# Attention and two expert layers on one core: the first batch's gate spread over two more background steps, the first slot's weight load tied to it

## The chip, the cores and the metric

The program runs on one core of a Trainium2 chip. The metric is the device time of one execution in microseconds (us); lower is better. The kernel before was run three times: 547.34, 546.74 and 547.10 us, median 547.1 us.

Engine names: PE is TensorE (PEld its weight loads), DVE is VectorE, ACT is ScalarE, POOL is GpSimd, SP is SyncE, which here issues the DMAs.

## The reference, cut to what matters

For 4 batches (B), 8 heads, 576 positions and head size 64, three layers follow each other:

```
phi(x) = [exp(p), exp(-p)],  p = x @ w_phi - max|x @ w_phi|      # 128 features, 256 with both signs
num = phi(q) @ (phi(k).T @ v);  den = phi(q) . sum_s phi(k);  x1 = num / den

logits = x1 @ w_gate                       # 4 experts, the 2 best of each position are used
x2 = sum over the 2 best e of  w_e * ( causal_softmax(q_e k_e^T / 8) v_e  @ wo_e )

e(s) = argmax of 8 logits, or the expert of the position before where a local gate says so
out = p[e] * relu(x2 @ w1[e]) @ w2[e]
```

The change lies in the first layer's end and in the gate of the second: for each batch the gate finds each position's two best experts of four, counts how often each expert is chosen in the batch, and orders the experts by their counts. The two experts with the highest counts get a full pass over the batch (a "slot").

## The kernel before, in words

**Phase A** computes the first layer. A unit is a batch and a pair of heads: 16 units, unit 4b + p for batch b and pair p. `PhaseA.run` (line 398) has 18 iterations, and iteration i works on three units at once: it projects the keys and queries of unit i (`proj`, line 223, tiles `pjk`, `pjq`, `pje`), makes features, transposes and the key-value product of unit i-1 (`feat_q`, `kv`, `keys`, lines 276 to 307, tiles `tr`, `Y`, `kvt`), and finishes unit i-2 (`num` and `den`, lines 330 and 347, tiles `pn`, `pd`; `den` only in odd iterations). The transposes of `kvtrans` (line 309) of units i-2 and i-1 use the same PSUM bank as `Y`, so that bank must be copied out in turn: line 307 copies Y, line 324 copies its transpose to `kvs`. The order inside an iteration is written out by hand:

```
A_STEPS = ("k0 e0 q0 t x0 f0 t f1 t a kv0 kv1 A t kv2 kv3 t n0 n1 z0 a t t A s0 d0 d1 t")     # line 36
```

Here k, e, q are the projections, x is `kvtrans`, f `feat_q`, kv the key-value product, n `num`, z `feat_k` (the exponentials of the keys on ACT and their sums on POOL), s `keys`, d `den`. Each `t`, and the end of the iteration, is one **tick**. An iteration has nine ticks, so iteration i holds ticks 9i + 1 to 9i + 9.

**Background work.** `Background` (line 69) holds generators in lanes. On each tick, each lane runs one step of its first generator, that is, up to the next `yield`; `yield n` lets the generator sleep until n ticks later, and an entry with `after` waits until the named entry is used up. The lanes of a tick run in the order of their names, "r" before "w". A step that is "held" gets an ordering edge: each of its instructions stands, on its own engine, behind the last anchor of that engine, which for DVE is the last subtraction of `proj` (line 250) and for ACT the last exponential of the features (lines 268, 284).

The code's order is not yet the order on an engine: the build orders the instructions of each engine within the data dependences, the order edges and the waits for buffers. Tiles with one tag share a few buffers in turn; the tag `mm` has two PSUM banks, which `pje`, `pn`, `pd`, the gate's logits (`pg`) and the gate's sum (`pc`) take one after the other.

When unit 4b + 3 is finished, `done(b)` (line 1663) adds to lane "r": `fin{b}` (line 363: store and reload the denominators, a reciprocal on DVE at line 371, reload them spread over the partitions, and eight products on POOL at line 390 that make x1 final) and `gate{b}` (line 1042: store x1 to memory, sleep, `Gates.top2`, store the weights `ws`). For batch 1 it adds to lane "w" the first slot's `early` (line 1174: two indices cast at line 656 and read by SP, two loads `wr` and two loads `wor` at lines 1121 and 1124, then the split of x1[0] into two parts, on ACT at line 1163 and DVE at line 1164) and `cast_w` (line 1126: three pairs of casts, ACT at line 1138 and DVE at line 1139, of the loaded `wr`).

`top2` (line 490) makes the logits in two steps, transposes them in two more, then the maximum, the comparisons (lines 506 to 509), and the choice and its counts `cnt` (lines 512 to 516). After a sleep the matmul at line 519 sums the counts over the partitions into `pc`. The next steps make the total (line 529), the order of the experts (`by_use`, lines 477 to 487, giving `perm`) and the weights in that order (lines 536 and 539, giving `ws`).

The ticks that follow from this:

| Step | Tick before | Iteration, place |
|---|---|---|
| batch 0: logits, first half | 77 | 8, fifth |
| batch 0: counts | 83 | 9, second |
| batch 0: sum `pc` | 85 | 9, fourth |
| batch 0: `perm`, then `ws` | 89, 90 | 9, eighth and ninth |
| slot 0: load, split, casts | 90; 91, 92; 94 to 96 | 9 and 10 |
| `fin1`: first step, reciprocal, products | 93; 97; 102 to 105 | 10 and 11 |
| batch 1: store of x1, logits | 107; 116 | 11; 12, eighth |
| batch 1: counts, sum `pc` | 122; 124 | 13, fifth and seventh |

The first slot's projections with the cast weights begin in iteration 16. **Phases B and C**, the second and third layers, follow phase A and are not touched.

Of the kernel before, what the change touches and what calls it, by code (L numbers as in the profile page):

```python
# [440 lines left out]
class Gates:  # L441
# [5 lines left out]
    def t(self, shape, tag, b, bufs=1, dt=F32):  # L447
        return self.wk.tile([128] + list(shape), dt, tag=tag, name=f"{tag}_{b}", bufs=bufs)
# [41 lines left out]
    def top2(self, xf, wg32, b, out):  # L490
# [10 lines left out]
        w = t([QT, 4], "w4", b)  # L501
# [12 lines left out]
        nc.vector.memset(sel[64:128, 4, :], 0.0)  # L514
        cnt = t([4], "cnt4", b)
        nc.vector.tensor_reduce(cnt, sel.rearrange("p t e -> p e t"), axis=AX.X, op=OP.add)
        yield 2
        pc = ps.tile([128, HALF], F32, tag="mm", name=f"pc_{b}")
        nc.tensor.matmul(pc[:, 0:4], k.ones, cnt, start=True, stop=True)
        nc.vector.tensor_tensor(w, w, sel, op=OP.mult)  # L520
# [490 lines left out]
class PhaseB:  # L1011
# [30 lines left out]
    def gate(self, b):  # L1042
        nc = self.nc
        g = self.g[b] = {}
        nc.sync.dma_start(self.x1d[b], self.x1[b])
        yield 9
        yield from self.gt.top2(self.x1[b], self.wg, b, g)
        nc.sync.dma_start(self.wsd[b], g["ws"])

        t = self.gt.t([2, 4], "ext", b)  # L1050
        nc.vector.tensor_tensor(t, g["hot"][:, 2:4], g["tot"][:, None, :].to_broadcast([128, 2, 4]), op=OP.mult)
        nc.vector.tensor_reduce(self.use[:, b], t, axis=AX.X, op=OP.add)
        nc.vector.tensor_copy(self.ex[:, 1, b], g["perm"][:, 2:4])
        yield
# [573 lines left out]
def kern(tc, kq, v, w_phi, b_gate, wqkv, wo, c_gate, w1, w2, out):  # L1628
    nc = tc.nc
    with ExitStack() as ctx:  # L1630
# [14 lines left out]
        bg = Background(tc)  # L1645
# [10 lines left out]
        with ExitStack() as c2:  # L1656
            ps.pool = c2.enter_context(tc.tile_pool(name="ps_a", bufs=2, space=PSUM, reuse_waits="tile"))
            ps.same = {"tr": ("X", 5), "X": ("X", 5)}
            pa = PhaseA(c2, tc, k, ps, gk, dr, hl, kq, v, w_phi, x1_tile, bg)
            pb.pools(wp, None, ps, None)  # L1660
            slots = pb.slots(order)

            def done(b):
                if b == 1:
                    bg.add("early_" + slots[0].nm, slots[0].early(), lane="w")
                    bg.add("cast_" + slots[0].nm, pb.cast_w(slots[0]), lane="w")
                fin = pa.fin(b)
                bg.add(f"fin{b}", fin, b < B - 1, lane="r", wait=(next(fin) if b == B - 1 else 0))
                bg.add(f"gate{b}", pb.gate(b), lane="r")
                if b == B - 2:  # L1670
                    bg.add("extras", pb.extras(), lane="r")

            pb.fronted = 4
            fronts = iter(range(pb.fronted))

            def after():
                for j in fronts:
                    if j == 0:
                        bg.ensure("cast_" + slots[0].nm)
                    slots[0].front(j)  # L1680
                    break

            def gate_weights():
                for o, w in ((pb, pb.w_gate), (pc, pc.w_gl)):
                    nc.sync.dma_start(o.wg[:, :, 0:w.shape[2]], w)
                    yield

            bg.add("wg", gate_weights())
            pa.run(done, after)
        ps.same = {}  # L1690
        ps.pool = ctx.enter_context(tc.tile_pool(name="ps", bufs=2, space=PSUM, reuse_waits="tile"))
# [66 lines left out]
```

## Time and profile before

| | us |
|---|---|
| median of three runs | 547.1 |
| lowest and highest run | 546.74, 547.34 |
| the profiled execution | 547.5 |
| its span, from first to last instruction | 545.6 |
| PE busy | 524.7 (96% of the span) |
| DVE busy | 362.3 (66%) |
| ACT busy | 263.8 (48%) |
| POOL busy | 157.8 (29%) |

The profile is one execution of the program, recorded by the hardware. Times count from the first instruction. A timeline row gives the start in us, the duration in us, the engine, the line of the kernel, the operation, its output and inputs by name with their shapes, and how many instructions the row merges; a bracket at its end gives the time that the engine sat idle just before, and what released it. Phase A takes about the first 165 us of the span.

### The profile page before, as it was taken

What the parts mean: (1) busy time and instruction counts of PE and PEld (TensorE: products, weight loads), DVE (VectorE), ACT (ScalarE), POOL (GpSimd) and SP (SyncE); (2) the same over time, 40 slices, a digit from 0 to 9 for tenths busy, and PEclk for the clock granted to TensorE, in tenths of its full rate; (3) what the DMA queues carried; (4) which work ended last, traced back from release to release, by engine and by line L of the source; (5) the groups of instructions that cost most, each with busy time, mean ns of one, the idle gap of its engine ahead of it and who ended that gap; (6) DMA issues with size and microseconds to landing.
All of it is one profiled execution on the core that took longest, in us unless ns stands there. A gap on an engine that the chain in (4) does not pass through costs nothing.

```text
span 545.6 us, 11798 instructions
## 1 busy us (share of the span) xinstructions
PE 524.7 (96%) x4456; PEld 439.5 (81%) x4456; DVE 362.3 (66%) x970; ACT 263.8 (48%) x603; POOL 157.8 (29%) x270
## 2 busy tenths in 40 slices
PE   6999999999999999999899999999999999999995
PEld 5776765666667687778667788999999999999995
DVE  7767677977763787968896866852665375617441
ACT  3748466665565466858646553430451135115100
POOL 5574696398468141112445100000000000000000
PEclk9999999999999999999999999999999999999998
DMA  8424364444016023501000601172335133813011
GB/s 245 132 73 127 87 219 135 148 149 157 27 37 217 5 68 115 207 1 55 26 1 2 233 0 31 49 251 107 126 121 193 45 127 122 281 43 126 2 48 46
DMA packets 32709, 57.07 MB, mean 105 GB/s; under 512 B 7012, under 2 KB 17636, under 8 KB 31620
## 3 DMA queue, kind: packets, MB, share of 16 engines
q1 hardware_dynamic: 32644, 56.24, 31.6%
q8 instruction: 37, 0.61, 0.5%
q14 instruction: 28, 0.23, 0.1%
HBM read 41.86 MB, written 14.36 MB: 103 GB/s over the span
## 4 chain that ended last, share of the span: by engine, by line
PE 73%; DVE 10%; ACT 8%; issue 3%; DMA 2%; POOL 2%; SPq 0%; ACTq 0%; DVEq 0%; POOLq 0%
PE po_c L64 6%; PE po_c L65 6%; PE po_c L66 6%; PE pq_s L724 6%; PE ph_c L64 5%; PE ph_c L66 5%; PE ph_c L65 5%; PE Y L295 4%; PE pd L357 3%; PE py_s L870 3%; PE pn L340 3%; PE pt_s L843 2%; PE pjk L242 2%; PE pg L458 2%; ACT a_kp L267 2%
## 5 line engine op out<-in xcount | busy, mean ns | idle before, releaser
L1441 ACT ACTIVATE h_c<-ph_c 128x288 fp32r<-128x288 f32 x64 | 26.0, 409 | 106.3 <-PE ph_c L66 106.0
L64 PE MATMUL ph_c<-xh_c,w1h_c 128*128 128x288 f32 x256 | 76.7, 300 | 0.0
L64 PE MATMUL po_c<-h_c,w2h_c 128*128 128x288 f32 x256 | 76.2, 298 | 0.0
L66 PE MATMUL ph_c<-xh_c,w1l_c 128*128 128x288 f32 x256 | 75.5, 296 | 0.3 <-DVE w1l_c L1394 0.3
L65 PE MATMUL ph_c<-xl_c,w1h_c 128*128 128x288 f32 x256 | 75.7, 296 | 0.0
L65 PE MATMUL po_c<-h_c,w2h_c 128*128 128x288 f32 x256 | 75.5, 295 | 0.0
L66 PE MATMUL po_c<-h_c,w2l_c 128*128 128x288 f32 x256 | 75.4, 294 | 0.0
L272 POOL TENSOR_TENSOR zs<-a_kp 128x256 f32<-128x256 f32 x64 | 47.6, 759 | 56.0 <-ACT x L345 29.0
L1442 DVE SCALAR_TENSOR_TENSOR h_c<-ph_c,h_c 128x288 fp32r<-128x288 f32 x64 | 28.9, 454 | 34.1 <-ACT h_c L1441 33.6
L64 PEld LDWEIGHTS ph_c<-xh_c,w1h_c 128*128 128x128 f32 x256 | 48.1, 188 | 1.6 <-issue 0.9
L64 PEld LDWEIGHTS po_c<-h_c,w2h_c 128*128 128x128 f32 x256 | 48.2, 188 | 0.9 <-issue 0.9
L66 PEld LDWEIGHTS ph_c<-xh_c,w1l_c 128*128 128x128 f32 x256 | 48.0, 188 | 0.9 <-issue 0.5
L65 PEld LDWEIGHTS ph_c<-xl_c,w1h_c 128*128 128x128 f32 x256 | 48.1, 188 | 0.0
L66 PEld LDWEIGHTS po_c<-h_c,w2l_c 128*128 128x128 f32 x256 | 48.1, 188 | 0.0
L65 PEld LDWEIGHTS po_c<-h_c,w2h_c 128*128 128x128 f32 x256 | 48.1, 188 | 0.0
L1464 DVE TENSOR_TENSOR fo_c<-po_c,pb 128x288 f32<-128x288 f32 x32 | 14.5, 455 | 45.3 <-PE po_c L66 45.2
L724 PE MATMUL pq_s<-xh_b,w_s 128*128 128x288 f32 x192 | 43.7, 305 | 0.7 <-DVE q_s L691 0.7
L295 PE MATMUL Y<-a_kp,a_v 128*64 128x256 f32 x320 | 39.3, 385 | 1.0 <-ACT qp L328 0.5
L340 PE MATMUL pn<-qp,kvs 128*64 128x288 f32 x256 | 35.9, 408 | 0.3 <-ACT qp L328 0.3
L267 ACT ACTIVATE a_kp<-uk 128x1024 f32<-128x1024 f32 x30 | 31.5, 1052 | 7.3 <-DVE uk L250 4.1
L724 PEld LDWEIGHTS pq_s<-xh_b,w_s 128*128 128x128 f32 x192 | 32.0, 188 | 3.1 <-issue 1.5
L284 ACT ACTIVATE qp<-tr 128x512 f32<-128x512 f32 x64 | 33.6, 634 | 1.3 <-PE tr L282 1.3
(315 smaller groups left out, 1218.2 us busy)
## 6 DMA issues: line engine op xcount, KB each, us to landing
w1raw_c<-in_w_dram SPq DMA_DIRECT2D x16, 512.0 KB, 4.2
w2raw_c<-in_w_dram SPq DMA_DIRECT2D x16, 512.0 KB, 4.5
raw<-in_kq_dram SPq DMA_DIRECT2D x15, 320.0 KB, 3.1
rb<-d SPq DMA_DIRECT2D x32, 144.0 KB, 3.4
x1d<-x SPq DMA_DIRECT2D x4, 1152.0 KB
x2d<-x SPq DMA_DIRECT2D x4, 1152.0 KB
raw<-in_kq_dram SPq DMA_DIRECT2D x16, 256.0 KB, 3.8
a_v<-in_v_dram SPq DMA_DIRECT2D x16, 256.0 KB, 4.1
```

What stands on the lines that cost most here:

```text
L64: nc.tensor.matmul(out, lh, rh, start=start, stop=False, **kw)
L65: nc.tensor.matmul(out, lh, rl, start=False, stop=False, **kw)
L66: return nc.tensor.matmul(out, ll, rh, start=False, stop=stop, **kw)
L267: nc.scalar.activation(kp[:, 0:4, sg, :], u[:, 0:4, :], AF.Exp, scale=sc)
L272: add(zs[:, j, sg, :], kp[:, j, sg, :], kp[:, 2 + j, sg, :], op=OP.add)
L284: self.bg.anchor(nc.scalar.activation(qp[:, h, sg, 0:512], tp, AF.Exp, scale=sc))
L295: self.kv_last = nc.tensor.matmul(Y[64 * h:64 * h + 64, 0:256], vt[:, t, h, :], kp[:, t, :, h * NF:(h + 1) * NF], start=t == 0, stop=t == 4)
L340: nc.tensor.matmul(pn[64 * h:64 * h + 64, :], kvs[:, sg, 64 * h:64 * h + 64], qp[:, h, sg, c], start=sg == 0, stop=sg == 1)
L357: nc.tensor.matmul(pd[32 * h:32 * h + 32, :], r["kvs"][:, 2, o:o + 32], r["qp"][:, h % 2, sg, c], start=sg == 0, stop=sg == 1)
L724: self.nc.tensor.matmul(out, self.wqkv[t][:, wj, ch, 0:m], x[:, ch, c], start=wj == ch == 0 and x is xh, stop=wj == 1 and ch == 3)
L1441: nc.scalar.activation(hh[:, c], ph, AF.Relu),
L1442: nc.vector.scalar_tensor_tensor(hl[:, c], ph, 0.0, rd(hh[:, c]), op0=OP.max, op1=OP.subtract))
```

## The change

Three lines change. Batch 0's gate sleeps four ticks instead of two between its counts and their sum. The first slot's `early` gets an `after` on gate 0, so it starts in the tick in which that gate is used up, where it had started on its own in tick 90. Batch 1's gate sleeps seven ticks instead of nine after its store of x1.

```
 # Gates.top2
         nc.vector.tensor_reduce(cnt, sel.rearrange("p t e -> p e t"), axis=AX.X, op=OP.add)
-        yield 2
+        yield 2 if b else 4
         pc = ps.tile([128, HALF], F32, tag="mm", name=f"pc_{b}")
         nc.tensor.matmul(pc[:, 0:4], k.ones, cnt, start=True, stop=True)
 # PhaseB.gate
         nc.sync.dma_start(self.x1d[b], self.x1[b])
-        yield 9
+        yield 7 if b == 1 else 9
         yield from self.gt.top2(self.x1[b], self.wg, b, g)
 # kern, done(b)
                 if b == 1:
-                    bg.add("early_" + slots[0].nm, slots[0].early(), lane="w")
+                    bg.add("early_" + slots[0].nm, slots[0].early(), lane="w", after=["gate0"])
                     bg.add("cast_" + slots[0].nm, pb.cast_w(slots[0]), lane="w")
```

The ticks after the change, where they differ:

| Step | Before | After |
|---|---|---|
| batch 0: sum `pc` | 85 | 87 |
| batch 0: total, order of the experts (three steps) | 86, 87 to 89 | 88, 89 to 91 |
| batch 0: `ws`; its store and the last small steps; used up | 90; 91; 92 | 92; 93; 94 |
| slot 0: load | 90 | 94 |
| slot 0: split, two steps | 91, 92 | 95, 96 |
| slot 0: casts, three steps | 94, 95, 96 | 98, 99, 100 |
| `fin1`: first step; reciprocal; products | 93; 97; 102 to 105 | 95; 99; 104 to 107 |
| batch 1: store of x1 | 107 | 109 |
| batch 1: logits and all that follows | 116 | 116 |

## Rows read from the trace of the kernel before

**Rows 1.** The page's first part: engine, busy us, share of the span, instructions

```profile
PE 524.7 (96%) x4456; PEld 439.5 (81%) x4456; DVE 362.3 (66%) x970; ACT 263.8 (48%) x603; POOL 157.8 (29%) x270
```

**Rows 2.** Busy time by stretch: length, then PE, PEld, DVE, ACT, POOL, clock, DMA

```profile
90.00:100.00 10.00, 8.99 (x98) 5.05 (x96) 9.02 (x33) 7.33 (x15) 7.59 (x11) 1.00 0.31 92
...
100.00:110.00 10.00, 9.96 (x109) 7.41 (x105) 9.80 (x22) 7.18 (x15) 1.10 (x2) 1.00 0.65 199
```

**Rows 3.** Waits of PE, 80 to 140 us: total us, times, longest

```profile
PE pc L519 <- DVE cnt L516: 1.0, 1, 1.0
PE pje L242 <- DVE x L343: 0.6, 1, 0.6
```

**Rows 4.** Timeline of PE, 93 to 100 us: start, us, instruction [idle before]

```profile
93.58 0.94 PE L242 MATMUL pjk<-a_w,raw 64*128 64x128 f32 x12
95.49 0.39 PE L519 MATMUL pc<-cnt,ones 128*128 128x4 f32 x2 [0.96 <-DVE cnt L516]
95.80 2.16 PE L340 MATMUL pn<-qp,kvs 128*64 128x288 f32 x16
...
100.06 0.49 PE L242 MATMUL pjk<-a_w,raw 64*128 64x128 f32 x4
```

**Rows 5.** Timeline of PE, batch 1's pc in iteration 13

```profile
140.47 0.39 PE L519 MATMUL pc<-cnt,ones 128*128 128x4 f32 x2
```

**Rows 6.** Timeline of DVE, 97 to 111 us

```profile
97.39 0.61 DVE L485 TENSOR_TENSOR u<-hot,iota 128x16 f32<-128x16 f32 x1
...
98.34 0.19 DVE L656 CAST ri_b<-perm 1x1 int32<-1x1 f32 x2
...
99.14 0.46 DVE L359 TENSOR_SCALAR dn<-pd 128x288 f32<-128x288 f32 x1 [0.24 <-PE pd L357]
100.20 0.46 DVE L359 TENSOR_SCALAR dn<-pd 128x288 f32<-128x288 f32 x1 [0.60 <-PE pd L357]
...
104.97 1.27 DVE L250 TENSOR_TENSOR uq<-pjq,mxq 128x512 f32<-128x512 f32 x2
...
107.05 2.08 DVE L1164 TENSOR_TENSOR xl_b<-x,xh_b 128x576 fp32r<-128x576 f32 x3
109.06 1.28 DVE L1139 TENSOR_TENSOR w_s<-wr_s,w_s 128x512 fp32r<-128x512 f32 x2
110.26 0.45 DVE L343 COPY x<-pn 128x288 f32<-128x288 f32 x1
```

**Rows 7.** Timeline of PE, 110 to 112 us

```profile
110.76 0.37 PE L242 MATMUL pje<-a_w,raw 64*128 64x128 f32 x1 [0.63 <-DVE x L343]
...
111.85 0.44 PE L318 MATMUL kvt<-ident,ue 128*128 128x128 f32 x2
```

**Rows 8.** Timeline of ACT, 102 to 113 us

```profile
102.82 0.49 ACT L324 ACTIVATE kvs<-kvt 128x384 f32<-128x384 f32 x1 [4.80 <-PE kvt L323]
...
104.48 1.29 ACT L1163 ACTIVATE xh_b<-x 128x576 fp32r<-128x576 f32 x2
...
106.58 1.20 ACT L1138 ACTIVATE w_s<-wr_s 128x512 fp32r<-128x512 f32 x2
...
110.41 0.64 ACT L1138 ACTIVATE w_s<-wr_s 128x512 fp32r<-128x512 f32 x1
110.93 0.49 ACT L307 ACTIVATE kvt<-Y 128x384 f32<-128x384 f32 x1
112.65 0.49 ACT L324 ACTIVATE kvs<-kvt 128x384 f32<-128x384 f32 x1 [1.23 <-PE kvt L323]
```

**Rows 9.** Timeline of SP's DMA issues near 100 us

```profile
100.49 0.90 SPq L1121 DMA_DIRECT2D wr_s<-in_wqkv_dram  x2
```

**Rows 10.** The tile wr_s: its eight loads, from issue to landing

```profile
DMA to landing us min/median/max: 3.1/3.3/3.7
```

**Rows 11.** Timeline of POOL (GpSimd), 127 us

```profile
126.97 1.55 POOL L390 TENSOR_TENSOR x<-x,rb 128x288 f32<-128x288 f32 x2
```

**Rows 12.** Timeline of PE, batch 1's logits

```profile
129.08 1.18 PE L458 MATMUL pg<-x,b_wg 128*32 128x288 f32 x16
```

More of the change, by code (lines that the diff above doesn't have):

```diff
@@ L516, in top2 @@
         nc.vector.tensor_reduce(cnt, sel.rearrange("p t e -> p e t"), axis=AX.X, op=OP.add)
-        yield 2
+        yield 2 if b else 4
         pc = ps.tile([128, HALF], F32, tag="mm", name=f"pc_{b}")
@@ L1045, in gate @@
         nc.sync.dma_start(self.x1d[b], self.x1[b])
-        yield 9
+        yield 7 if b == 1 else 9
         yield from self.gt.top2(self.x1[b], self.wg, b, g)
@@ L1664, in done @@
                 if b == 1:
-                    bg.add("early_" + slots[0].nm, slots[0].early(), lane="w")
+                    bg.add("early_" + slots[0].nm, slots[0].early(), lane="w", after=["gate0"])
                     bg.add("cast_" + slots[0].nm, pb.cast_w(slots[0]), lane="w")
```

## The prediction, made before the changed kernel was run

> **What bounds the kernel now.** Read the page's first part first: TensorE (PE) is busy for 524.7 of the 545.6 us span [rows 1], so a change pays only where it removes a wait of PE, and the 20.9 us without PE work are all there is. The profiled execution took 547.5 us: its span and 1.9 us around it, 0.4 us above the median of 547.1. The sum below is made against 547.5 and then carried to the median.
>
> Next, the table by stretches. The change touches batch 0's gate and what follows it, and these lie at 90 to 110 us: PE 8.99 and 9.96 of 10 us, VectorE (DVE) 9.02 and 9.80 [rows 2]. DVE is nearly full too, so what PE waits for there is DVE. The list of waits names PE's only two large ones between 80 and 140 us: 1.0 us for the counts (cnt, line 516) and 0.6 us for a PSUM copy (line 343) [rows 3].
>
> PE's timeline shows the first. Instructions don't stand in the code's order: the build orders each engine's list. Twelve of unit 10's sixteen key matmuls come at 93.58, ahead of unit 7's numerators (pn), since pn takes the `mm` bank after the sum's (pc). PE idles 0.96 us before pc at 95.49; pn follows at 95.80, and the last four key matmuls at 100.06 [rows 4].
>
> **The change, step by step.** Iteration i of phase A holds ticks 9i+1 to 9i+9; batch 0's counts are made in tick 83.
>
> *Step 1: pc from tick 85 (between the products of keys and values) to tick 87 (after pn).* pn now asks for its bank first, and its inputs are there, so its 2.1 us run while DVE finishes cnt. The key matmuls go back behind; nothing is added. Gain 0.96 us; bounds 0 (a new wait for the same cnt) and 0.96. The nearest row for the new place is batch 1's pc, already issued from its iteration's seventh tick: no idle time of PE before it [rows 5]. Can DVE follow? It idles 0.24 and 0.60 us just before unit 10's reductions, and the last of the gate's small steps (perm, ws, the two index casts), 97.39 to 98.53, fill 1.14 us [rows 6]. These go to ticks 91 to 94, where a held step stands behind unit 10's last subtraction, so DVE has 0.84 + 1.14 us to give and PE's 0.96 us stand: that subtraction ends about 105.2 instead of 106.2.
>
> The Trainium skill (Trace Analysis, "Identifying Performance Opportunities") says to look for gains on the engine with the highest occupancy. Over this stretch DVE nearly ties with PE, and by that rule step 1 would be worth DVE's idle time alone, some 0.84 us. The idle rows agree with the size; no run here separates 0.84 from 0.96.
>
> *Step 2: x1's split from ticks 91, 92 to 95, 96; the weight casts from 94 to 96 to 98 to 100.* In the old order unit 8's PSUM copy (line 343, 110.26) stands behind four subtractions of the split and two of the casts: the three at 107.05 and the two at 109.06 alone take 2.08 + 1.28 us [rows 6]. PE idles 0.63 us for it at 110.76 [rows 7]. In the new order only two split subtractions are ahead of it: about 105.2 + 1.1 (moved gate work) + 1.4 + 0.45 = 108.2, before PE asks (110.13 - 0.96 = 109.2). Gain 0.63; bounds 0 and 0.63.
>
> *Step 3: what is late next, ScalarE (ACT).* Unit 9's transposes (line 318) began at 111.85 [rows 7], just behind ACT's copy of Y (line 307), 110.93 to 111.42, which must drain that bank. ACT ran without a hole from unit 8's kvs copy at 102.82 to the end of that copy, 8.6 us, with two split copies (1.29) and three casts (1.20 + 0.64) among it [rows 8]. In the new order all four split copies (2.58) and no cast stand in this run, so it is 0.55 us shorter, and it starts 0.96 earlier: it ends at 111.42 - 0.96 - 0.55 = 109.9 if no hole opens. But the second pair of split copies (tick 96) now stands directly ahead of the copy, behind the key exponentials, where before one cast of 0.64 did, so the end may slip by as much as 1.29 - 0.64 = 0.65, to 110.55. PE would come at 111.85 - 1.59 = 110.26. The bounds of the wait are so 0 and 0.3; I take 0.25, near the upper, since the split copies rank ahead of that copy in the code.
>
> *Step 4: the loads.* Slot 0's load goes from tick 90 to 94. Its index casts ended at 98.53; the two `wr` loads took SP from 100.49 to 101.39, the second begun about 2.4 us after the casts [rows 9], and land 3.1 to 3.7 us after issue [rows 10]. From the end of the subtraction: 105.2 + 1.14 to the casts + 2.4 to the second load + 3.1 to 3.7 = 111.8 to 112.4. On SP, behind the wait for the index, stand slot 0's four loads, batch 1's denominators (tick 95 instead of 93) and unit 13's load, which PE wants in iteration 13; the denominators go into DVE's reciprocal of tick 99 (97 before). I price SP at 0 to PE. The slots' first use of the weights is in iteration 16: 0. Unit 9's kvs copy (ACT, 112.65 with 1.23 us idle ahead of it [rows 8]) is wanted at once by PE. If the casts stay behind it, 0: ACT then has the query copies and casts to do before PE needs unit 9's products copied, and the next iteration is the light kind. If not, rival B.
>
> *Step 5: batch 1.* Its fin moves two ticks, its gate's store of x1 as much (109 for 107), its logits stay in tick 116. The store's bytes are unchanged and the loads behind it in SP are for units 14 and 15: 0, with the margin in rival D.
>
> **Sum:** -0.96 - 0.63 + 0.25 = **-1.3 us**: 546.2 for the profiled execution, **545.8** against the median. After phase A nothing else changes; the later waits are set by the same engines and move along.
>
> **Rivals.**
>
> *A: only one of the two waits goes.* If the build leaves the second pair of split subtractions ahead of line 343's copy as well, PE waits there as before and step 2 is worth 0. Step 3 then takes nothing, since PE comes later: -0.96, **546.1**. For it: DVE and ACT are full here [rows 2, 8], so work that is moved four ticks stands in front of something. Against: the new ticks lie, in the code, behind the copies that PE wants.
>
> *B: the weight casts stop ACT; slower.* Ticks 98 to 100 come ahead of iteration 11's kvs copy in the code. If the build puts the casts there, ACT's list stands until the weights land (111.8 to 112.4), then runs one to three casts of 0.6 us, then kvs. One cast gives kvs at 112.4 to 113.0 against 112.65 now, about no change; two give 113.0 to 113.6 and three 113.6 to 114.2, a loss of 1.0 to 1.6: **548.1 to 548.7**. From the second cast on the kernel is slower than before. (The same casts' subtractions, ahead of unit 11's reductions on DVE, would hold PE's products of unit 9 by as much.) For it: the old order put a cast ahead of the Y copy at 110.41 [rows 8]. Against: the build had the freedom to leave them to the next iteration.
>
> *C: nothing moves.* pc is still early for cnt, or the hole comes back as another wait: **547.1**.
>
> *D: batch 1's logits wait for GpSimd.* The last scaled half of x1 ends at 128.52 [rows 11], PE's logits start at 129.08 [rows 12]. The margin is 0.56; GpSimd's work moves with ACT's products, so mostly 0, but one pair of products (1.55) put later costs 1.55 - 0.56 = 1.0 of what was won: **546.8**.
>
> **How the numbers follow.** About 0.2% (1.1 us) is what a measurement of this kernel can tell from no change: faster means under 546.0, slower over 548.2. Forecast 0.46 (545.8, its own range 545.5 to 546.2; of it 0.41 faster, 0.05 same), A 0.22 (0.03 faster, 0.19 same), B 0.20 (0.15 slower, 0.05 same), C 0.06 and D 0.06 (same). That makes faster 0.44, same 0.41, slower 0.15. The range runs from the whole 1.59 us less half the spread of the three runs (0.3) to B with three casts at the early landing and a little more: 545.2 to 548.2.
>
> **What would show it.** Step 1: pn directly after the products, pc without idle time, unit 10's key matmuls unsplit. Step 2: no wait of PE for line 343. Step 3: PE's wait, if any, is at line 318 for line 307, under 0.4 us. Step 4: the `wr` loads near 108.5, casts behind kvs. It is wrong if ACT shows a wait for wr ahead of kvs (B), if pc still idles (C), or if PE waits for line 390 (D); and if the time goes outside 90 to 135 us, the order of some other stage has changed, which I have not priced.

## The result and the profile after

The changed kernel took 551.1 us (median of five runs, 550.75 to 552.41), beside 547.34 us for the kernel before on the same chip (five runs, 546.74 to 547.88): a ratio of 1.0066, with an interval of 1.0046 to 1.0085. It is **slower by 0.66%, 3.8 us by the medians**. The forecast was 1.3 us faster, and the range ended at 548.2.

The page's first part, the row that answers to [rows 1] (engine, busy us, share of the span, instructions), and the granted clock in 40 slices of the span:

```profile
PE 525.4 (96%) x4456; PEld 439.5 (80%) x4456; DVE 363.9 (66%) x970; ACT 263.6 (48%) x603; POOL 157.3 (29%) x270
...
PEclk9999999979999999999999999999999999999999
```

The span grew from 545.6 to 549.3 us, by 3.7 us. The sums of the engines hardly differ (PE +0.7 us, with the same 4456 instructions), so the reader has to look along the span. One slice stands out, the ninth (109.9 to 123.6 us): its digit of the granted clock is 7, and all others are 9.

**Where the time went** is best read from PE's own marks. Each column below runs from the first row of a group on PE's timeline to the first of the next: the second half of batch 0's logits (pg), the first key matmul (pjk) of units 11, 12 and 13, and the first matmul of the second layer (pq).

| us | pg to unit 11 | unit 11 to 12 | 12 to 13 | 13 to pq | pg to pq | pq to the end |
|---|---|---|---|---|---|---|
| before | 23.53 | 12.09 | 9.79 | 33.87 | 79.28 | 381.54 |
| changed | 22.35 | 17.40 | 9.79 | 33.87 | 83.41 | 381.49 |

So the change won 1.18 us up to unit 11, lost 5.31 in the one iteration behind it, and did nothing to the rest. The sum is +4.13. With -0.38 ahead of the first mark, where the change does nothing, and -0.05 behind the last, that is the span's 3.70 us.

PE's timeline through these stretches (start us, us, instruction, idle time before it and what ended it), the rows that answer to [rows 4, 7]:

```profile
92.74 2.11 PE L340 MATMUL pn<-qp,kvs 128*64 128x288 f32 x16
...
95.32 0.39 PE L519 MATMUL pc<-cnt,ones 128*128 128x4 f32 x2
...
106.75 1.16 PE L242 MATMUL pjk<-a_w,raw 64*128 64x128 f32 x16
...
109.51 0.44 PE L318 MATMUL kvt<-ident,ue 128*128 128x128 f32 x2 [0.48 <-ACT kvt L307]
...
111.81 0.63 PE L282 MATMUL tr<-ident,uq 128*128 128x128 f32 x4 [1.09 <-DVE uk L250]
114.95 4.53 PE L295 MATMUL Y<-a_kp,a_v 128*64 128x256 f32 x20 [2.52 <-ACT qp L328]
119.27 2.65 PE L340 MATMUL pn<-qp,kvs 128*64 128x288 f32 x16
...
124.15 1.16 PE L242 MATMUL pjk<-a_w,raw 64*128 64x128 f32 x16
```

The two waits aimed at are gone: pn stands ahead of pc, pc has no idle time, and line 242 no longer waits for line 343. In their place stand 1.09 us for DVE and 2.52 us for ACT. The twenty matmuls behind them, Y at 114.95, take 4.53 us; the same twenty took 2.38 in the iteration before, at 102.15. ACT's timeline, the rows that answer to [rows 8], shows the 2.52:

```profile
108.96 0.50 ACT L307 ACTIVATE kvt<-Y 128x384 f32<-128x384 f32 x1
112.52 1.67 ACT L1138 ACTIVATE w_s<-wr_s 128x512 fp32r<-128x512 f32 x3 [3.06 <-DMA wr_s<-in_wqkv_dram]
114.10 0.47 ACT L324 ACTIVATE kvs<-kvt 128x384 f32<-128x384 f32 x1
114.47 0.43 ACT L328 ACTIVATE qp<-kvt 128x128 f32<-128x128 f32 x2
```

All three weight casts stand ahead of unit 9's kvs copy, and ACT does nothing for 3.06 us until the weights land. The kvs copy starts at 114.10, where it started at 112.65 before. The load itself, on SP's timeline (it answers to [rows 9]; the last row is the store of batch 1's reciprocals, which stands behind slot 0's four loads):

```profile
107.71 0.90 SPq L1121 DMA_DIRECT2D wr_s<-in_wqkv_dram  x2
...
110.09 0.53 SPq L373 DMA_DIRECT2D d<-cr  x1
```

DVE's timeline, which answers to [rows 6], shows the 1.09:

```profile
103.84 1.27 DVE L250 TENSOR_TENSOR uq<-pjq,mxq 128x512 f32<-128x512 f32 x2
...
105.70 0.20 DVE L656 CAST ri_b<-perm 1x1 int32<-1x1 f32 x2
105.83 1.41 DVE L1164 TENSOR_TENSOR xl_b<-x,xh_b 128x576 fp32r<-128x576 f32 x2
107.16 0.44 DVE L343 COPY x<-pn 128x288 f32<-128x288 f32 x1
...
108.56 2.50 DVE L1164 TENSOR_TENSOR xl_b<-x,xh_b 128x576 fp32r<-128x576 f32 x2
110.98 0.68 DVE L250 TENSOR_TENSOR uk<-pjk,mxk 128x512 f32<-128x512 f32 x1
...
113.18 1.79 DVE L1139 TENSOR_TENSOR w_s<-wr_s,w_s 128x512 fp32r<-128x512 f32 x2 [0.93 <-ACT w_s L1138]
```

The index casts come 7.4 us later than before (98.34 to 105.70), because the step that holds them now lies in iteration 10 and stands behind unit 10's last subtraction (uq, 103.84). The second pair of the split stands ahead of unit 11's uk, and takes 2.50 us where the first pair took 1.41.

Last, the granted clock. The view by stretches (length; busy us of PE, PEld, DVE, ACT and POOL; then clock, DMA share, GB/s):

```profile
110.00:112.00 2.00, 0.91 (x9) 0.70 (x8) 2.00 (x3) 0.00 (x0) 2.00 (x3) 1.00 1.05 342
112.00:114.00 2.00, 0.43 (x4) 0.19 (x2) 1.07 (x2) 1.48 (x3) 1.74 (x3) 0.89 0.85 275
114.00:116.00 2.00, 1.05 (x6) 0.67 (x8) 2.00 (x6) 2.00 (x7) 0.00 (x0) 0.50 0.50 176
116.00:118.00 2.00, 2.00 (x14) 1.05 (x12) 2.00 (x5) 0.84 (x2) 0.87 (x2) 0.50 0.71 226
118.00:120.00 2.00, 2.00 (x12) 1.18 (x10) 1.35 (x3) 1.19 (x2) 0.68 (x1) 0.50 0.24 73
120.00:122.00 2.00, 2.00 (x20) 0.92 (x20) 0.03 (x1) 1.72 (x4) 0.00 (x0) 0.91 0.78 177
```

PE is busy 0.91 and 0.43 of 2 us, and then the clock stands at 0.50, the lower of its two levels (1.2 GHz), until about 120 us. Y and pn are issued in that stretch. From the start of Y to the end of pn, 114.95 to 119.27 + 2.65 = 121.92, they take 6.97 us; before, 113.53 to 117.85, 4.32. That is 2.65 us for the same 36 matmuls. PE's timeline of the kernel before:

```profile
113.53 2.38 PE L295 MATMUL Y<-a_kp,a_v 128*64 128x256 f32 x20
115.74 2.11 PE L340 MATMUL pn<-qp,kvs 128*64 128x288 f32 x16
```

So the +5.31 us of the iteration come apart in three: from unit 11's first matmul to the start of Y 8.20 us instead of 5.22 (+2.98), the clock +2.65, and a smaller gap behind pn (-0.32).

### The profile page after: what moved, and what is told of

Read it like the earlier page. It is cut to its first block, busy times and chain, and to the rows that moved or that the text cites. A ratio compares the mean times of both kernels' runs of the same rounds, so it can differ in the third digit from the quotient of the medians.

```text
span 549.3 us, 11798 instructions
## 1 busy us (share of the span) xinstructions
PE 525.4 (96%) x4456; PEld 439.5 (80%) x4456; DVE 363.9 (66%) x970; ACT 263.6 (48%) x603; POOL 157.3 (29%) x270
## 4 chain that ended last, share of the span: by engine, by line
PE 78%; DVE 7%; ACT 7%; issue 3%; DMA 3%; POOL 2%; SPq 0%; ACTq 0%; POOLq 0%; DVEq 0%
PE po_c L64 6%; PE po_c L65 6%; PE po_c L66 6%; PE pq_s L724 6%; PE Y L295 5%; PE ph_c L64 5%; PE ph_c L66 5%; PE ph_c L65 5%; PE pn L340 3%; PE py_s L870 3%; PE pd L357 3%; PE pjk L242 3%; PE pt_s L843 2%; PE pg L458 2%; ACT a_kp L267 2%
## 5 line engine op out<-in xcount | busy, mean ns | idle before, releaser
L295 PE MATMUL Y<-a_kp,a_v 128*64 128x256 f32 x320 | 41.4, 401 | 3.6 <-ACT qp L328 3.2
L295 PEld LDWEIGHTS Y<-a_kp,a_v 128*64 128x64 f32 x320 | 22.7, 142 | 17.6 <-ACT qp L328 7.0
```

Source lines behind the costliest of these rows:

```text
L295: self.kv_last = nc.tensor.matmul(Y[64 * h:64 * h + 64, 0:256], vt[:, t, h, :], kp[:, t, :, h * NF:(h + 1) * NF], start=t == 0, stop=t == 4)
```

## The experiments

The theory after this reading was: the bound load is late, the casts stand ahead of kvs on ACT, PE's wait is long, and the wait also lowers PE's clock. The rivals were that DVE alone would hold PE, that the clock costs nothing of its own, and that batch 1's gate, begun two steps sooner, is what loses. Each experiment is an edit of the changed kernel unless another base is named. Where marks are given, they are those of the table above. `wait=n` in an edit holds an entry back until n ticks after the one in which it is added, tick 89.

### The casts alone put later

```
-                    bg.add("cast_" + slots[0].nm, pb.cast_w(slots[0]), lane="w")
+                    bg.add("cast_" + slots[0].nm, pb.cast_w(slots[0]), lane="w", wait=14)
```

> The changed kernel, with slot 0's three weight casts asked for nine ticks after the load (tick 103) instead of from tick 98 on; the order of ACT differs only in that. Theory T (the casts stand ahead of unit 9's kvs copy on ACT and hold it until the weights have landed; PE idles, then its clock falls): kvs follows PE's transposes at once, PE's 2.5 us wait and the 2.65 us of half clock go. What stays is the gain at pc and PE's 0.5 and 1.1 us waits at lines 318 and 282: about 547.1, 546.3 to 547.7. Rival U (the loss comes from DVE, where the split's second pair stands ahead of unit 11's subtraction): PE's 1.1 us wait grows and the time stays above 549.

Measured: 548.23 us (ten runs, 546.98 to 550.06) beside 547.62; ratio 1.0009, interval 0.9997 to 1.0022. Against the changed kernel's 1.0066 that undoes most of the loss, though not down to the range expected. PE's timeline of this run:

```profile
111.92 0.63 PE L282 MATMUL tr<-ident,uq 128*128 128x128 f32 x4 [1.07 <-DVE uk L250]
112.48 2.38 PE L295 MATMUL Y<-a_kp,a_v 128*64 128x256 f32 x20
...
129.27 1.43 PE L458 MATMUL pg<-x,b_wg 128*32 128x288 f32 x10 [0.83 <-POOL x L390]
```

Y starts at 112.48, has no wait for ACT and takes 2.38 us; the granted clock is 1.00 in every 2-us stretch from 110 to 122. Unit 11 to 12 takes 12.14 us instead of 17.40. So the casts ahead of kvs are the loss of that iteration. DVE's 1.07 us is still there, and Y nevertheless starts 1.05 us sooner than in the kernel before (113.53).

What is left is new: unit 12 to 13 takes 11.60 us instead of 9.79, because the logits of batch 1 wait for GpSimd: from their first matmul to unit 13 it takes 2.92 us (127.71 to 130.63) where it took 1.11. The chain begins on POOL's timeline. The products with the reloaded reciprocals start only at 117.81, after 3.86 us of waiting for their data:

```profile
117.81 2.09 POOL L390 TENSOR_TENSOR x<-x,rb 128x288 f32<-128x288 f32 x2 [3.86 <-DMA rb<-d]
```

The small store of the reciprocals is issued at 110.23, behind slot 0's four loads, and SP then waits 2.3 us for its landing before it may reload them. In the changed kernel the same products start at 117.13 and cost nothing, since PE itself is some 4 us late there. This is the prediction's rival D: covered in the changed kernel, real as soon as the first loss is gone.

### Casts of data that are ready

Slot 0's casts read the finished x1 of batch 0 in place of the loaded weights, so they don't wait for the load; slot 0's output is then that of other weights.

```
                 src = s.wr[:, :, :, 64 * t:64 * t + 64].rearrange("p j c d -> p c j d")
+                if nm == "s0":
+                    src = self.x1[0][:, :, 0:384].rearrange("p c (j d) -> p c j d", j=2)[:, :, :, 64 * t:64 * t + 64]
```

> The changed kernel in its own order of instructions, but slot 0's casts read x1 of batch 0, which is in place, instead of the loaded weights (slot 0 computes with other numbers, so the output is not the reference's). The loads still run. T: the casts run at about 109.5 to 111.2 and kvs at about 111.2 instead of 114.1, so Y of unit 10 waits for its transposes alone; clock stays at 1.0; 547.0 to 547.8. Rival W (it is the three casts' own 1.7 us on ACT, or their place, not the waiting for the load): kvs late by 1.7 us and more, 549 or above.

Measured: 550.15 us (four runs), ratio 1.0044, interval 1.0028 to 1.0061. **A miss.** kvs starts at about 110.9 as foreseen, and ACT's wait is gone, but PE waits for DVE instead:

```profile
113.96 0.66 PE L282 MATMUL tr<-ident,uq 128*128 128x128 f32 x4 [1.57 <-DVE uk L250]
114.54 3.84 PE L295 MATMUL Y<-a_kp,a_v 128*64 128x256 f32 x17
```

On DVE's timeline two of the casts' subtractions now follow the second pair of the split, all ahead of unit 11's uk:

```profile
108.53 2.49 DVE L1166 TENSOR_TENSOR xl_b<-x,xh_b 128x576 fp32r<-128x576 f32 x2
110.94 2.36 DVE L1141 TENSOR_TENSOR w_s<-x,w_s 128x512 fp32r<-128x512 f32 x2
113.23 0.68 DVE L250 TENSOR_TENSOR uk<-pjk,mxk 128x512 f32<-128x512 f32 x1
```

Y starts at 114.54 instead of 114.95, and the clock falls here as well (0.68, then 0.50 from 116 to 118). So a loss of this kind comes without the wait for the load, from the place of the casts alone: held by the load they stop ACT, and not held they fill DVE at the same place. The prediction had this second path in brackets under rival B.

### PE kept busy in the gap

Unit 10's query transposes are repeated, two and four times in all, so that PE has work while it would wait.

```
-        for t in range(4):
+        for t in list(range(4)) * ((2, 4)[h] if i == 10 else 1):
```

> The changed kernel, with the query transposes of unit 10 done over again (the first four twice, the second four four times, same result), so that PE has some 2 us of work in the hole ahead of unit 10's Y; the wait of ACT for the weights is untouched. T with the clock as a part of the loss: granted clock stays near 1.0 after the hole, Y takes 2.4 us instead of 4.5, and the time falls by 1.5 to 2.7 us to 548.4 to 549.6. If the half clock comes from elsewhere or costs nothing: no change, 550.7 to 551.6.

Measured: 551.06 us (four runs), ratio 1.0063, interval 1.0045 to 1.0081: no gain in the total that the runs can tell. The price of the clock is seen all the same. PE's timeline and the view by stretches:

```profile
115.88 2.38 PE L295 MATMUL Y<-a_kp,a_v 128*64 128x256 f32 x20 [1.35 <-ACT qp L328]
118.09 2.11 PE L340 MATMUL pn<-qp,kvs 128*64 128x288 f32 x16
```

```profile
114.00:116.00 2.00, 0.65 (x7) 0.41 (x7) 1.89 (x3) 2.00 (x7) 0.63 (x1) 1.00 0.51 185
116.00:118.00 2.00, 2.00 (x20) 1.35 (x22) 2.00 (x7) 1.77 (x4) 0.00 (x0) 1.00 0.64 211
```

Y starts later than in the changed kernel (115.88 instead of 114.95), and Y and pn are still done sooner (at 120.20 instead of 121.92): they take 4.32 us at a clock of 1.00, exactly what they took before the change, against 6.97. From pg to pq the stretch takes 81.22 us, 2.19 less than the changed kernel's 83.41. In the profiled run 1.1 us of that are given back behind pq (382.59 instead of 381.49); of it, 0.68 us is a wait at 224 us for a split copy on ACT (line 1163) that the changed kernel's profile does not show. Behind pq, where the code is the same in all, this record's thirteen traces range from 381.49 to 383.09, so 1.1 us there need not come from this edit. So the local cost of the clock is shown, and that its removal lowers the total is not.

### Batch 1's gate put back

```
-        yield 7 if b == 1 else 9
+        yield 9
```

> The changed kernel with the third edit undone: batch 1's gate sleeps nine ticks again, so its logits and what follows come two ticks later than before. T: the loss was made before tick 109, so 550.5 to 551.7. Rival V (the shorter sleep of batch 1's gate costs, through its store or its logits waiting for GpSimd): at least 1 us faster, 550 or below.

Measured: 552.65 us (four runs), ratio 1.0091, interval 1.0074 to 1.0108. That is above the range expected and not below it, so the third edit is not the loss. Without it the stretch from unit 12 to pq takes 44.76 us instead of 43.66, and the logits come later and with a wait:

```profile
136.26 1.18 PE L458 MATMUL pg<-x,b_wg 128*32 128x288 f32 x16 [0.89 <-DVE ue L250]
```

The two steps taken from that sleep keep the gate in its old ticks once `fin1` has moved by two. What they are worth is not shown: unit 11 to 12 is 1.07 us shorter here (16.33 instead of 17.40, with a clock that falls less, to 0.57 and 0.58), so pg to pq takes 83.45 us against 83.41. The totals of this run and of the changed kernel overlap in their intervals.

### The binding alone

The kernel before, with the second edit only.

```
-                    bg.add("early_" + slots[0].nm, slots[0].early(), lane="w")
+                    bg.add("early_" + slots[0].nm, slots[0].early(), lane="w", after=["gate0"])
```

> Edit: the kernel before with only the second edit of the change, slot 0's load bound to the first gate. T (the binding is what moves the casts ahead of kvs): all three casts in a row ahead of unit 10's kvs copy, PE idle there by 2 us or more, the granted clock below 1.00 behind it; 549 to 551 us. Rival U (the binding costs only together with the later counts): casts find their data, kvs late by at most 0.6, 547.0 to 548.0.

Measured: 550.66 us (five runs, 548.86 to 552.98), ratio 1.0053, interval 1.0033 to 1.0074: as expected. The load, the index casts and the casts move by two ticks only, from 90 to 92, but that takes them from iteration 9 into iteration 10. There the index casts stand behind unit 10's last subtraction on DVE (106.24 us instead of 98.34), and the load is issued at 108.53 instead of 100.49. This run's timelines of ACT and then of PE:

```profile
114.34 1.67 ACT L1138 ACTIVATE w_s<-wr_s 128x512 fp32r<-128x512 f32 x3 [3.40 <-DMA wr_s<-in_wqkv_dram]
115.92 0.47 ACT L324 ACTIVATE kvs<-kvt 128x384 f32<-128x384 f32 x1
```

```profile
116.77 3.91 PE L295 MATMUL Y<-a_kp,a_v 128*64 128x256 f32 x20 [3.50 <-ACT qp L328]
```

The clock is 0.50 from 118 to 120 us. From unit 11 to the last twelve key matmuls of unit 12 (four went ahead, at 112.57) it takes 16.77 us against 12.09 before, and from pg to pq 83.86 against 79.28. One `after` of two ticks gives a loss of this size by itself, and with nothing won ahead of it. Note DVE: here it waits 2.84 us itself, and both of unit 11's uk subtractions are done in time. So DVE's 1.09 us of the changed kernel is beside the point, and ACT's stop is enough.

The trace is of an execution of 552.70 us, 2.0 above the median. The five differ in their mean granted clock as they do in time: 548.86 us at 0.999, 550.66 and 550.58 at 0.996 and 0.995, 552.70 and 552.98 at 0.994 and 0.992. The first, whose clock is as high as the kernel before has it, is 1.1 us above the 547.76 us of the kernel before, which is the size that the prediction gave to rival B.

The first edit has no run without the second, since `early` on its own starts in tick 90 and reads the weights `ws`, which the first edit moves from tick 90 to 92.

### The changed kernel again

> The changed kernel, unaltered, on the same chip as the runs of this group, to have its trace a second time. T: three casts ahead of unit 10's kvs, first pjk of unit 12 about 17.4 us behind that of unit 11 (12.1 in the kernel before), granted clock at 0.50 for some us around 116; 550.7 to 551.8 us.

Measured beside the last one: 551.87 us (four runs, 551.7 to 553.62), ratio 1.0084, interval 1.0069 to 1.0099, just above the range, with the same waits (unit 11 to 12 in 17.95 us, Y at 115.64 after 3.04 us for ACT, and a clock of 0.57, 0.50, 0.50 and 0.72 from 114 to 122). The whole change is no faster than its second edit alone, although its first wins 1.2 us ahead of unit 11.

### Load, split and casts all put a unit later, on both kernels

If the preparation of slot 0 only has to be away from units 10 and 11, putting it a unit later should keep steps 1 and 2 and lose nothing. In ticks of the changed kernel, this edit puts the load from 94 to 103, one iteration later at the same place, and the casts from 98 to 113, one iteration and six ticks later; the same waits on the kernel before put them from 90 and 94 to the same ticks. On the changed kernel:

```
-                    bg.add("early_" + slots[0].nm, slots[0].early(), lane="w", after=["gate0"])
-                    bg.add("cast_" + slots[0].nm, pb.cast_w(slots[0]), lane="w")
+                    bg.add("early_" + slots[0].nm, slots[0].early(), lane="w", after=["gate0"], wait=14)
+                    bg.add("cast_" + slots[0].nm, pb.cast_w(slots[0]), lane="w", wait=24)
```

> Edit: the changed kernel with slot 0's load (and with it the split) 14 background steps later and its casts 24 steps later, so that all of it falls one unit later, at the same place within the unit, and the load stands on SyncE behind the reciprocals rb of the second batch instead of ahead of them. Theory T (the changed kernel loses because slot 0's preparation stands in the wrong places: casts ahead of unit 10's kvs copy, the load in flight beside the reciprocals' way): no cast ahead of kvs of unit 10 or 11, GpSimd's first multiply by rb starts at 113 to 115 (117.1 in the changed kernel, 117.8 with the casts alone later), no wait of the second batch's logits for GpSimd, first pjk of unit 12 at 118.5 to 119.3, clock 1.00 throughout; 545.8 to 546.8 us, about 0.25% faster than before. Rival P (GpSimd's own work and not the load sets the second batch's logits): the wait of 0.8 us at the logits stays, 547.4 to 548.2. Rival Q (unit 13's input loads, now behind slot 0's load on SyncE, are late): PE waits for raw at pjk of unit 13, 548 or more.

and the same two waits on the kernel before:

> Edit: the kernel before with slot 0's load and split 14 steps later and its casts 24 steps later; its first batch's counts and the second batch's gate stay where they were. T: the wait of 0.96 us at pc stays, the 0.63 us at pje for the x copy goes, first pjk of unit 12 at 119.7 to 120.2; 546.5 to 547.3 us, so the run above is faster than this one by 0.5 to 1 us. Rival S (the counts' later place is worth nothing, all of the gain is in slot 0's places): equal to the run above within 0.3 us.

Measured: 548.68 us (eleven runs), ratio 1.0019, interval 1.0009 to 1.0029; and 549.05 us (twelve runs), ratio 1.0022, interval 1.0008 to 1.0037. **Both are misses.** They differ by 0.37 us, less than the 0.5 expected, and their intervals overlap, so they do not show what the counts' later place is worth. In the first, unit 11 to 12 takes 10.44 us instead of 12.09, and the next two stretches pay for it, with 12.55 and 35.42 us. PE's waits there:

```profile
119.57 0.37 PE L242 MATMUL pje<-a_w,raw 64*128 64x128 f32 x1 [0.98 <-DVE dn L359]
...
128.44 0.31 PE L304 MATMUL Y<-zs,ones 128*32 128x128 f32 x3 [1.22 <-POOL zs L274]
...
132.60 0.37 PE L242 MATMUL pje<-a_w,raw 64*128 64x128 f32 x1 [1.47 <-DVE lg L459]
```

The waits of 0.98 and 1.47 us are the old line 343's kind: a PSUM bank that DVE has not emptied, with subtractions of the preparation ahead on DVE (those of the split at 117.06 take 2.09 us, a single one of a cast at 125.01 takes 2.78). So the preparation has a price here too.

### The load behind the reciprocals, the casts late

Next, two arrangements that use what was learnt. The first puts the split where the change has it (one tick sooner, since the load no longer takes the tick ahead of it), the load at tick 104 instead of 94, behind the reciprocals' round trip, and the casts at 130 instead of 98:

```
         def early():
+            if b == 0:
+                yield from self.split(lambda ch: self.x1[b][:, ch, :], q, f"b{b}", s.xs)
+                yield 8
             self.load_w(...)
             yield
-            yield from self.split(lambda ch: self.x1[b][:, ch, :], q, f"b{b}", s.xs)
+            if b:
+                yield from self.split(lambda ch: self.x1[b][:, ch, :], q, f"b{b}", s.xs)
...
-                    bg.add("cast_" + slots[0].nm, pb.cast_w(slots[0]), lane="w")
+                    bg.add("cast_" + slots[0].nm, pb.cast_w(slots[0]), lane="w", wait=41)
```

> Edit: the changed kernel, with slot 0's split where the change put it, but its load behind the second batch's reciprocals rb on SyncE and its casts three units later (unit 13 in place of unit 10). Theory T2 (two prices make up the loss: the casts ahead of unit 10's kvs with the slow clock behind it, and the load, in flight while the reciprocals make their round trip, which makes GpSimd's multiplies late): with both removed the 1.2 us won at the counts are kept. Expected: pc and the x copy without a wait, first pjk of unit 11 at 22.3 to 22.4 us behind the first pg (as in the changed kernel), first multiply by rb by 115, no wait at the second batch's logits, first pjk of unit 13 at 43.8 to 44.6 us behind the first pg (45.4 before, 46.1 with the casts alone later, 49.5 in the changed kernel); 546.2 to 547.0 us, 0.1 to 0.3% below before. Rival P2 (GpSimd's own work is the limit, whenever the load comes): the wait at the logits stays at 0.5 us or more, 547.3 to 548.2. Rival C2 (the casts cost as much in unit 13 as elsewhere): a wait of 1 us or more behind them, 547.5 or more.

Measured: 547.11 us (twelve runs), ratio 0.9996, interval 0.9983 to 1.0009. From pg to unit 13 it takes 44.13 us, inside the range expected and 1.28 us less than before (45.41), with no wait at the logits. The wait for the x copy of line 343, expected to stay away, is there (0.75 us at 108.89). The rest gives 0.94 back and puts the total just above its range: unit 13 to pq takes 34.81 us, and PE waits 0.86 us for uk at 154.53, beside the three casts that now follow each other at 147 to 152 us.

### The split two units later, too

The second keeps the load ahead of the split: the load at tick 103, the split at 121, the casts at 130, which are iterations 11, 13 and 14:

```
-            yield
+            yield 18 if b == 0 else 0
...
-                    bg.add("early_" + slots[0].nm, slots[0].early(), lane="w", after=["gate0"])
-                    bg.add("cast_" + slots[0].nm, pb.cast_w(slots[0]), lane="w")
+                    bg.add("early_" + slots[0].nm, slots[0].early(), lane="w", after=["gate0"], wait=14)
+                    bg.add("cast_" + slots[0].nm, pb.cast_w(slots[0]), lane="w", wait=41)
```

> Edit: as the run above, with the split, too, two units later than in the changed kernel, in unit 12, so that units 10 and 11 hold no preparation of slot 0 at all. T2 with GpSimd as the next limit: units 11 and 12 begin about 1.6 us sooner than in the run above, but GpSimd's eight multiplies by rb then stand ahead of unit 12's sums and PE waits for those by 1 to 2.5 us, so that the logits come no sooner than 128.2: first pjk of unit 13 at 44.8 to 45.4 us behind the first pg; 546.5 to 547.6 us. Rival F (what counts is only that units 10 and 11 are free): the 1.6 us are kept, 544.6 to 545.4.

Measured: 547.8 us (eleven runs), ratio 0.9999, interval 0.9991 to 1.0008. Units 11 and 12 are the shortest together (pg to 13 in 42.89 us), and unit 13 to pq takes 36.20 instead of 33.87, with waits of 0.59 us for dn and 0.85 us for uk. No gain in sum, and a miss for both: unit 13 comes sooner than T2 had it and without its wait for GpSimd, and what rival F would keep is lost behind it.

### One cast a unit

Last, the arrangement with the late load, with its three casts an iteration apart:

```
             nc.vector.tensor_tensor(l, src, rd(h), op=OP.subtract)
-            yield
+            yield 9 if s.nm == "s0" else 0
...
-                    bg.add("cast_" + slots[0].nm, pb.cast_w(slots[0]), lane="w", wait=41)
+                    bg.add("cast_" + slots[0].nm, pb.cast_w(slots[0]), lane="w", wait=32)
```

> Edit: as the run with the load behind rb, with the three casts spread, one in each of units 12, 13 and 14, each behind the copies of the query features' transposes. T2: the wait of 0.86 us of unit 15's transposes for DVE (three subtractions close together) goes, and what was won up to unit 13 stays: first pjk of unit 13 at 44.0 to 44.4 us behind the first pg, first pq of phase B 33.8 to 34.3 us behind that (33.87 before, 34.81 with the casts together), so 77.9 to 78.7 from the first pg to phase B (79.28 before); 546.2 to 546.9 us, 0.15 to 0.3% below before. Rival C3 (each cast costs its own time on DVE, wherever it stands): 34.8 or more behind unit 13, 547 or more.

Measured: **546.49 us** (eleven runs, 545.83 to 547.03) beside 547.76; ratio 0.9978, interval 0.9969 to 0.9987. It is faster than both kernels, by 0.22% than the one before, and each part is in the range expected: pg to 13 in 44.13 us, 13 to pq in 33.88, in all 78.01 against 79.28 before. The load stands behind the reload of the reciprocals on SP, and the casts' subtractions stand alone on DVE (SP's and DVE's timelines):

```profile
110.75 6.33 SPq L380 DMA_DIRECT2D rb<-d  x8
119.00 1.32 SPq L1121 DMA_DIRECT2D wr_s<-in_wqkv_dram  x2
```

```profile
136.86 0.69 DVE L1139 TENSOR_TENSOR w_s<-wr_s,w_s 128x512 fp32r<-128x512 f32 x1
149.07 0.68 DVE L1139 TENSOR_TENSOR w_s<-wr_s,w_s 128x512 fp32r<-128x512 f32 x1
157.77 0.62 DVE L1139 TENSOR_TENSOR w_s<-wr_s,w_s 128x512 fp32r<-128x512 f32 x1
```

The first products on POOL start at 114.41, 2.7 us sooner than in the changed kernel. Of the waits that the prediction spoke of, line 343's is left (0.75 us at 109.01): all four subtractions of the split stand ahead of that copy, as rival A had it. That the split's one tick sooner does this is likely and not tested.

## Why the prediction was wrong, point by point

**What bounds the kernel: right.** PE's waits were what counted, and the loss is in PE's waits and in PE's clock.

The changed kernel's profile stands 0.38 us ahead before the change does anything, so its times below would be that much later on the clock of the times foreseen.

**Step 1: right.** pn went ahead of pc, pc shows no idle time, and DVE could follow: uq ends at 103.84 + 1.27 = 105.11, where 105.2 was said. One sign did not come: unit 10's key matmuls stayed split, four at 95.98 and twelve at 98.48, now around the denominators (pd). **Step 2: right.** Line 343's copy stands behind one pair of the split, at 107.16, and PE does not wait for it. From pg to unit 11, where 0.96 was foreseen (and 0.84 by DVE's idle time alone), the gain is 1.18 us; where the other 0.22 comes from was not traced. From pg to line 318 it is 27.07 - 25.11 = 1.96, where 1.34 was foreseen (step 3's wait taken off in both).

**Step 3: right in kind.** PE waits at line 318 for line 307, for 0.48 us, where 0 to 0.3 was the range and 0.25 was taken: PE came at 109.03, sooner than the 110.26 foreseen. ACT's copy ended at 108.96 + 0.50 = 109.46, sooner than the earlier of the two ends named (109.9).

**Step 4 failed:** "If the casts stay behind it, 0 ... If not, rival B." They did not stay behind it. The times of the step are nearly right: load at 107.71 (foreseen near 108.5), landing at 112.52 (111.8 to 112.4), three casts, kvs at 114.10 (113.6 to 114.2). So rival B happened as it was told, in its strongest form, and was given 0.20. The reason against it, that the build was free to leave the casts to the next iteration, had no row behind it. The reason for it had one: a cast ahead of the Y copy at 110.41 [rows 8]. The row should have counted for more.

**Rival B's price was also too small**: 1.0 to 1.6 us were foreseen, and 3.7 measured in the span. Its own term was about right: kvs starts 1.45 us later, and Y at 114.95 instead of 113.53, 1.42 us later (1.80 counted from pg). What it lacked is what PE's idle time does to PE's clock: 2.65 us on Y and pn. With -0.32 behind pn these make 3.75 at unit 12, the whole loss of the span (3.7). The Trainium skill (TensorE: Matmul & The Clock Gate, "HAM oscillation — how this bites in real kernels") says that a PE waiting for data falls back to half its rate, and that the next work starts slow. This trace agrees, with 2.65 us on 36 matmuls as the price of one such fall here. The prediction summed waits alone. Yet an idle time of about 2 us was in rival B's own working: PE at its transposes from 110.26, 1.7 us of them as before (111.85 to 113.53), and kvs at 113.6 to 114.2. The prediction did not ask what the clock does in such a hole. Its range also ended at 548.2, below rival B's own upper end.

**The binding was priced at nothing.** The late load was foreseen to within 1 us, and its lateness was held to cost 0, since the weights' first use by PE is in iteration 16. But the casts are a use too, and they stand in ACT's list ahead of work that PE wants at once. The run of the binding alone shows that this gives a loss of the whole size. It also shows that the count of ticks says little: two ticks, across the edge of an iteration, put the load 8.0 us later, and four ticks 7.2.

**Step 5 and rival D:** right that it costs nothing here, but for another reason than was given. PE's own lateness covers it. With the casts out of the way (the run with the casts alone put later) it cost PE 1.81 us at the logits, 0.83 of it in one wait, and unit 12 to 13 grew by that much.

**Rival A** (only one of the waits goes) is what the fastest arrangement shows: line 343's wait stays, 0.75 us, and step 1's goes. **Rival C** fell.

**What is not settled:** the run with PE kept busy shows the clock's price where it falls and does not show it in the total. The five executions of the binding alone point to it in the total, but they are no experiment on the clock. And which of the idle time's length and its place decides whether the clock falls was not tried by itself.

## What to carry to other kernels

An entry that waits for a load has no slack of its own on an engine that runs in order (ACT stood for 3.06 us here): what matters is what stands behind it in that engine's list, and when the load lands. So, before a load is put later, put its consumers later by more, and look which edge of an iteration the move crosses, not by how many steps it goes. When a rival holds PE idle for as long as here (2.5 to 3.5 us), price PE's clock as well, from rows at both levels. Preparation that fits nowhere as a lump may fit in single pieces: the same three casts cost 0.94 us together and nothing that the trace shows one by one.

## What the runs showed of the hardware that was not expected

**PE's clock falls in the middle of a busy kernel.** The granted clock fell to 0.50 in the runs where PE idled 2.52, 3.04 and 3.50 us ahead of Y (the changed kernel twice, and the binding alone), and also in the one with 1.57 us behind a wait of 1.05 us (casts of ready data). With 2.4 us (batch 1's gate put back) the lowest stretch shows 0.57. It stayed at 1.00 where the longest idle time was 1.07, 1.35 and 1.47 us (the casts alone put later, PE kept busy, all a unit later on the changed kernel). The fall showed as three stretches of 2 us at 0.50 in the changed kernel and one in the run with ready data.

**Subtractions on DVE take longer while GpSimd works.** The split's first pair took 1.41 us at 105.83, with POOL idle until 107.03; the second, of the same shape, 2.50 us at 108.56, with POOL's sums running without a hole (POOL's timeline of the changed kernel):

```profile
107.03 1.52 POOL L272 TENSOR_TENSOR zs<-a_kp 128x256 f32<-128x256 f32 x2 [5.09 <-PE Y L304]
...
110.40 1.94 POOL L272 TENSOR_TENSOR zs<-a_kp 128x256 f32<-128x256 f32 x2
```

POOL's own are longer too: 1.94 us for a pair where 1.52 stands above it. DVE's subtraction from PSUM (uk, line 250) kept its 0.68 us at 110.98. The Trainium skill (SBUF — State Buffer, "SBUF: two separate sides") says that an operation of DVE with two inputs in SBUF and one of GpSimd that reads SBUF share a pair of ports, which one of them holds for a whole instruction while the other stands still. The rows agree in kind: both engines get longer, and DVE's operation from PSUM does not. In the kernel before it was the other way about: the casts' two subtractions at 109.06 kept 0.64 us each [rows 6], and POOL's pair beside them took 2.48 (POOL's timeline of the kernel before):

```profile
109.15 2.48 POOL L272 TENSOR_TENSOR zs<-a_kp 128x256 f32<-128x256 f32 x2 [8.90 <-ACT a_kp L267]
```

**A small round trip waits behind a large load.** With slot 0's loads in flight (DMA share 1.05 and 0.85 of the engines' time from 110 to 114 us in the changed kernel), the first product with the reloaded reciprocals started at 117.13 and 117.81; with the load behind the round trip, at 114.41. From the store of the reciprocals to the start of their reload SP takes 3.14 us (110.09 to 113.23) and 3.80 (110.23 to 114.03) in the first two, 1.48 (109.27 to 110.75) in the last and 1.52 (111.02 to 112.54) in the kernel before. Whether the place in the queue or the busy DMA engines make it longer was not separated.
